# Token rows that move in 32-column groups: cluster similarities, softmax sums and gate logits of a routed-attention and expert kernel

## The chip, the cores and the metric

The kernel runs on one core of one Trainium2 chip. The metric is the device time of one launch in microseconds; lower is better. The core has TensorE (PE in the profile, with its weight loads as PEld), VectorE (DVE), ScalarE (ACT), GpSimd (POOL) and SyncE (SP, which issues most of the transfers). A program runs each engine's instructions in their written order. TensorE writes to PSUM, of which there are eight banks; the other engines copy from there.

## The reference

Two blocks follow each other. The first is attention with a mask from clustering: q, k and v have 4 batches, 8 heads, 768 tokens and 64 elements per head; each head has 16 centroids.

```
q_assign = argmax over c of  q_n . c_n      (k_assign likewise)
mask     = q_assign[:, None] == k_assign[None, :]
scores   = where(mask, q k^T / 8, -1e9);  attn = softmax(scores);  x = attn v
```

The second takes x as 3072 tokens of 512 elements and sends each to one of 8 experts:

```
logits = x @ w_gate                          (512 x 8)
e      = argmax(logits);  gate = softmax(logits)[e]
out    = gate * (relu(x @ w1[e]) @ w2[e])    (512 x 1024, 1024 x 512)
```

## The kernel before

All matrices are fp32. The attention stage works on 16 groups; a group is one batch and two heads, `a` = 0 and 1, which lie on partitions 0 to 63 and 64 to 127. A group has two halves of 384 queries, a half has six key blocks of 128, and a half with one key block is a unit: 12 units per group, 192 in all. `score(u)` computes the two heads' transposed scores of a unit (keys on partitions, 384 queries in the columns), adds the cluster mask by a bf16 product of one-hot tables, takes the exponential on ScalarE into `A`, and adds `A` into the sums tile `T` on VectorE. `attend(u)` multiplies `A` with v into the bank `O`, head `a` on partitions 64a to 64a+63.

The order is written out by hand. The loop steps two units at a time: two scores, two attends of two units earlier (LAG = 2), and then the jobs that a table `jobs` holds for the two units. A group's preparation begins 14 units ahead (LEAD): `turn` (three pieces of four transposes that bring q and k into `qk`, tokens in the columns), `similar` (the product with the normalized centroids, 12 matmuls, each with 128 tokens as the weights and 32 columns, so that tokens come out on partitions), `assign` and `assign2` (the first maximum as a one-hot row, on VectorE and GpSimd), `put` (six bf16 transposes for q and six for k, which bring the one-hot rows into `ohT`). `finish(g, half)` comes two units behind a half: it sums `T` over the keys with a matrix of ones, takes the reciprocal, multiplies `O` with it into `XT` (features on partitions, tokens in the columns), and adds up on GpSimd what a check of the range needs later. When the four groups of a batch are done, six `x_turn` jobs turn `XT` into token rows `X`, two `logits` jobs multiply `XT` with the gate matrix (12 matmuls each, 8 columns), `gate` computes the gate weight, and `keep_rows` writes the rows to DRAM from GpSimd's queue.

All jobs that need a PSUM bank for a short time take one of the two buffers called `mps` (pool `ps_m`); scores have four banks, `O` has two.

Behind the attention stage a chain of small VectorE operations and matmuls (from `sc`, L572, to `s_idx`, L676) sorts the tokens by expert. The expert stage gathers rows, turns them, and runs two layers per expert. The check of the range (L610 to L616) decides whether a general version of the whole kernel has to run behind this one; with the inputs here it does not.

Of the kernel before, what the change touches and what calls it, by code (L numbers as in the profile page):

```python
# [20 lines left out]
LAG = 2  # L21
# [161 lines left out]
def kernel(  # L183
# [11 lines left out]
    nc = tc.nc  # L195
    B, H, S, D = q.shape
    C = centroids.shape[1]
    P = 128
    NQ = S // P
# [10 lines left out]
    NT = N // P  # L210
    KA = D + C
    XW = Dm + 4
    assert D == 64 and H * C == P and NQ * P == S and DB * P == Dm and FB * P == F

    NJ = N // E // P
    CAP = NJ * P
# [30 lines left out]
    lmax = rte.tile([P, NT], F32)  # L247


    rsum = rte.tile([P, HS], F32)  # L250
    rlow = rte.tile([P, HS], F32)

    with ExitStack() as actx:
        ld = actx.enter_context(tc.tile_pool(name="ld", bufs=2))
# [7 lines left out]
        xtp = actx.enter_context(tc.tile_pool(name="xtp", bufs=5))  # L262
# [21 lines left out]
        wg = consts.tile([P, DB, E], F32)  # L284
        nc.scalar.dma_start(out=wg, in_=moe_w_gate.rearrange("(a p) e -> p a e", p=P))
# [6 lines left out]
        ones_h = consts.tile([P, D], F32)  # L292
        nc.gpsimd.memset(ones_h, 1.0)
        nc.gpsimd.memset(rsum, 0.0)
        nc.gpsimd.memset(rlow, 0.0)

        ohs = []
        for i in range(2):
# [52 lines left out]
                nc.scalar.copy(dst, src)  # L351

        def similar(g):
            ps = ps_m.tile([P, 512], F32, name="mps")
            for w in range(2):
                for j in range(NQ):
                    c0 = (w * NQ + j) * 2 * C
                    nc.tensor.matmul(  # L358
                        ps[:, c0 : c0 + 2 * C], lhsT=qk[g][:, w, j * P : (j + 1) * P],
                        rhs=cblk[:, g % HP].rearrange("p a c -> p (a c)"), start=True, stop=True,  # L360
                    )
            sims[g] = asg.tile([P, G, C], F32, name="sim")
            nc.scalar.copy(sims[g], ps[:, 0 : G * C].rearrange("p (t c) -> p t c", c=C))

        def assign(g):

            sim = sims.pop(g)
            mx = asg.tile([P, G], F32, name="mx")
            nc.vector.tensor_reduce(mx, sim, axis=AX, op=ALU.max)
            rank = asg.tile([P, G, C], F32, name="rank")  # L370
            nc.vector.tensor_tensor(rank, sim, mx.unsqueeze(2).to_broadcast([P, G, C]), op=ALU.is_ge)
            nc.gpsimd.tensor_tensor(rank, rank, first_c[:, None, :].to_broadcast([P, G, C]), op=ALU.mult)
            sims[g] = rank

        def assign2(g):
            rank = sims.pop(g)
# [7 lines left out]
        def put(g, w):  # L384
            if w == 0:
                ohT[g] = ohp.tile([P, 2, S], BF16, name="ohT")
            ps = ps_m.tile([P, 512], F32, name="mps").bitcast(BF16)
            for j in range(NQ):
                nc.tensor.transpose(
                    ps[:, j * P : (j + 1) * P], ohs[g % 2][:, w * NQ + j].rearrange("p a c -> p (a c)"), ident_b  # L390
                )
# [15 lines left out]
        def score(u):  # L407
            g, half, j = where(u)
            qs = slice(half * HS, (half + 1) * HS)
            ks = slice(j * P, (j + 1) * P)  # L410
            ps = ps_s.tile([P, 2, 512], F32, name="sps")
            for a in range(2):
                r = slice(a * D, (a + 1) * D)
                nc.tensor.matmul(ps[:, a, 0:HS], lhsT=qk[g][r, 1, ks], rhs=qk[g][r, 0, qs], start=True, stop=False)  # L414
            for a in range(2):
                r = slice(a * D, (a + 1) * D)
                nc.tensor.matmul(ps[:, a, 0:HS], lhsT=ohT[g][r, 1, ks], rhs=ohT[g][r, 0, qs], start=False, stop=True)  # L417
            A[u] = ap.tile([P, 2, HS], F32, name="A")
            nc.scalar.activation(A[u], ps[:, :, 0:HS], AF.Exp)  # L419
            if j == 1:  # L420
                T[g, half] = tp_.tile([P, 2, HS], F32, name="T")
                nc.vector.scalar_tensor_tensor(  # L422
                    T[g, half], in0=A[u - 1], scalar=1e-9 / P, in1=A[u], op0=ALU.add, op1=ALU.add
                )
            elif j > 1:
                nc.vector.tensor_tensor(T[g, half], T[g, half], A[u], op=ALU.add)  # L426
# [10 lines left out]
                )  # L437

        def finish(g, half):
            b, hp = divmod(g, HP)  # L440
            if half == 0:
                XT[b, hp] = xtp.tile([P, S], F32, name="xT")
            ps = ps_m.tile([P, 512], F32, name="mps")
            t = T.pop((g, half))
            for a in range(2):
                nc.tensor.matmul(  # L446
                    ps[a * D : (a + 1) * D, 0:HS], lhsT=ones_h, rhs=t[:, a, :], start=True, stop=True,
                )
# [10 lines left out]
        def x_turn(b, j):  # L459
            if j == 0:  # L460
# [3 lines left out]
            for c in range(DB):  # L464
                nc.tensor.transpose(ps[:, c * P : (c + 1) * P], XT[b, c][:, j * P : (j + 1) * P], ident)
            nc.scalar.copy(X[b][:, j, 0:Dm], ps)

        def logits(b, js):
            ps = ps_m.tile([P, 512], F32, name="mps")
            for i, j in enumerate(js):  # L470
                for c in range(DB):
                    nc.tensor.matmul(
                        ps[:, i * E : (i + 1) * E], lhsT=XT[b, c][:, j * P : (j + 1) * P], rhs=wg[:, c, :],
                        start=(c == 0), stop=(c == DB - 1),
                    )
            nc.vector.tensor_copy(
                lg[:, b * NQ + js[0] : b * NQ + js[-1] + 1, :],
                ps[:, 0 : len(js) * E].rearrange("p (j e) -> p j e", e=E),
            )

        def gate(b):
# [20 lines left out]
        def at(u, f, *a):  # L502
            jobs.setdefault(u, []).append((f, a))
# [3 lines left out]
        for g in range(NG):  # L507
            u0 = g * UG - LEAD
            for piece in range(3):
                at(u0 + piece, turn, g, piece)  # L510
            at(u0 + 4, similar, g)
            at(u0 + 5, assign, g)
            at(u0 + 7, assign2, g)
            at(u0 + 9, put, g, 0)
            at(u0 + 10, put, g, 1)
# [4 lines left out]
        for b in range(B):  # L520
            u0 = (b + 1) * HP * UG + LAG + 1
            for j in range(NQ):
                at(u0 + j, x_turn, b, j)
            at(u0 + 1, logits, b, (0, 1, 2))
            at(u0 + 3, logits, b, (3, 4, 5))
            at(u0 + 5, gate, b)
            at(u0 + 6, keep_rows, b)

        def early(e):
            weights[e] = fetch(e)  # L530
# [39 lines left out]
    with tc.tile_pool(name="sm", bufs=1) as sm, tc.tile_pool(name="rps", bufs=1, space=PSUM) as rps:  # L570
# [36 lines left out]
        )  # L607

        bad = sm.tile([P, 4], F32)
        nc.vector.tensor_reduce(bad[:, 0:1], rsum, axis=AX, op=ALU.max)  # L610
        nc.vector.tensor_reduce(bad[:, 1:2], rlow, axis=AX, op=ALU.max)
        nc.vector.tensor_scalar(bad[:, 0:1], bad[:, 0:1], scalar1=100.0, scalar2=None, op0=ALU.is_le)
        nc.vector.tensor_scalar(bad[:, 1:2], bad[:, 1:2], scalar1=0.5, scalar2=None, op0=ALU.is_le)
        nc.vector.tensor_tensor(bad[:, 2:3], bad[:, 0:1], bad[:, 1:2], op=ALU.mult)
# [187 lines left out]
```

## Time and profile before

| | us |
|---|---|
| median of three runs | 1006.79 |
| lowest and highest | 993.57, 1011.89 |
| the profiled execution, its own time | 1008.31 |
| its span in the trace | 1006.5 |
| attention stage, first score to last attend | 20.28 to 498.90 |
| last attend to the first routing operation (`sc`) | 498.90 to 515.64 |
| first weight load of the expert layers | 547.64 |

All times in the trace count from the start of the span. A fp32 matmul appears as two records of MATMUL, a fp32 transpose as one. Records of matmuls overlap, so the cost of a piece of PE work is best read from its start to the start of the next work of another kind. The granted clock is given as a share of TensorE's full speed (1.0 is 2.4 GHz, 0.5 is 1.2 GHz). A number in square brackets behind an instruction is the idle time of its engine ahead of it, and what ended that.

### The profile page before, as it was taken

The numbers are of one execution on the slowest core, as the hardware profiler recorded it, in microseconds if no ns is written. First come the engines' busy times: TensorE is split into PE (matmuls) and PEld (weight loads), VectorE is DVE, ScalarE is ACT, GpSimd is POOL, SyncE is SP. The second block draws the span as 40 slices with busy tenths as digits, with TensorE's granted clock in tenths as the row PEclk, the third lists the DMA queues.
The fourth block names the chain that finished last, engine by engine and source line by source line (L and its number), as shares of the span: only waits on it lengthen the run. The fifth ranks groups of instructions, "written<-read, shape, count | busy, mean of one in ns | idle before, by whom it ended". The sixth has DMA issues, their size and how long they took to land. (4 is left out here: it accounts for less than half of the span.)

```text
span 1006.5 us, 11290 instructions
## 1 busy us (share of the span) xinstructions
PE 941.5 (94%) x4655; PEld 525.4 (52%) x4655; DVE 386.2 (38%) x493; ACT 257.1 (26%) x392; POOL 210.8 (21%) x218
## 2 busy tenths in 40 slices
PE   5999999999999999999967999999999999988896
PEld 4555555454555555555365555545455454555664
DVE  2677745677447775477752101011010100000110
ACT  4444434444334443344410010101100010010100
POOL 3133321333113332132323020101201011010100
PEclk8999989999789998899955999999999999998998
DMA  7016223161221612100012242324334233446610
GB/s 166 16 41 214 49 48 109 32 199 35 48 80 32 215 48 48 73 7 1 1 63 64 83 145 97 133 105 160 141 128 146 100 131 125 159 165 223 236 62 9
DMA packets 82587, 99.02 MB, mean 98 GB/s; under 512 B 52959, under 2 KB 57055, under 8 KB 82016
## 3 DMA queue, kind: packets, MB, share of 16 engines
q1 hardware_dynamic: 76480, 77.60, 24.9%
q0 software_dynamic: 5376, 20.56, 5.2%
q8 instruction: 39, 0.64, 0.3%
q14 instruction: 20, 0.16, 0.1%
q10 hardware_dynamic: 672, 0.05, 0.0%
HBM read 85.57 MB, written 14.20 MB: 99 GB/s over the span
## 5 line engine op out<-in xcount | busy, mean ns | idle before, releaser
L706 PE MATMUL hp<-xgT,w 128*128 128x384 f32 (+1 forms) x896 | 212.9, 399 | 0.8 <-DVE xgT L698 0.8
L719 PE MATMUL zp<-w,h_sb 128*128 128x512 f32 x480 | 211.2, 599 | 0.0
L419 ACT ACTIVATE A<-sps 128x768 f32<-128x768 f32 x192 | 155.2, 811 | 110.9 <-PE sps L417 106.7
L414 PE MATMUL sps<-qk 64*128 64x384 f32 x768 | 183.1, 557 | 0.4 <-ACT A L419 0.4
L706 PEld LDWEIGHTS hp<-xgT,w 128*128 128x128 f32 x896 | 142.4, 193 | 74.2 <-issue 8.6
L426 DVE TENSOR_TENSOR T<-T,A 128x768 f32<-128x768 f32 x128 | 133.9, 1046 | 88.8 <-ACT A L419 82.7
L711 DVE TENSOR_SCALAR h_sb<-hp 128x384 f32<-128x384 f32 (+1 forms) x56 | 24.8, 444 | 359.2 <-PE hp L706 359.2
L434 PE MATMUL O<-A,v_in 128*64 128x384 f32 x768 | 149.7, 512 | 0.0
L719 PEld LDWEIGHTS zp<-w,h_sb 128*128 128x128 f32 x480 | 91.4, 193 | 109.8 <-issue 109.8
L725 POOL DMA_INDIRECT out_dram<-zo,s_idx x30 | 30.1, 1002 | 391.5 <-ACT zo L724 378.5
L454 POOL TENSOR_TENSOR rsum<-rsum,rd 128x384 f32<-128x384 f32 x32 | 32.0, 1000 | 333.0 <-DVE rd L450 333.0
L434 PEld LDWEIGHTS O<-A,v_in 128*64 128x64 f32 x768 | 48.4, 141 | 89.0 <-issue 88.9
L414 PEld LDWEIGHTS sps<-qk 64*128 64x128 f32 x768 | 69.6, 203 | 46.9 <-issue 25.6
L450 DVE RECIPROCAL rd<-mps 128x384 f32<-128x384 f32 x32 | 81.8, 2557 | 3.2 <-PE mps L446 2.1
L724 ACT ACTIVATE zo<-zp,xg 128x512 f32<-128x512 f32 x30 | 20.6, 687 | 222.1 <-PE zp L719 222.1
L713 ACT ACTIVATE h_sb<-hp 128x384 f32<-128x384 f32 (+1 forms) x56 | 22.3, 399 | 214.8 <-PE hp L706 214.8
L417 PE MATMUL sps<-ohT 64*128 64x384 bf16 x384 | 69.0, 352 | 0.0
L358 PEld LDWEIGHTS mps<-cblk,qk 128*128 128x128 f32 x384 | 44.3, 193 | 9.2 <-issue 9.2
L455 POOL TENSOR_SCALAR rd<-rd 128x384 f32<-128x384 f32 x32 | 45.9, 1433 | 2.8
L422 DVE SCALAR_TENSOR_TENSOR T<-A 128x768 f32<-128x768 f32 x32 | 31.2, 976 | 39.6 <-ACT A L419 39.6
L358 PE MATMUL mps<-cblk,qk 128*128 128x32 f32 x384 | 46.0, 278 | 0.0
L697 PE MATMUL tp<-ident,xg 128*128 128x128 f32 x120 | 19.3, 298 | 21.2 <-DMA xg<-x_rows,g_idx 18.8
(140 smaller groups left out, 556.0 us busy)
## 6 DMA issues: line engine op xcount, KB each, us to landing
w<-in_moe_w_dram SPq DMA_DIRECT2D x28, 2048.0 KB, 9.4
x_rows<-x POOLq DMA_DIRECT2D x4, 1548.0 KB, 5.5
q_in<-in_q_dram SPq DMA_DIRECT2D x32, 192.0 KB, 4.4
k_in<-in_k_dram SPq DMA_DIRECT2D x32, 192.0 KB, 4.7
v_in<-in_v_dram SPq DMA_DIRECT2D x16, 384.0 KB, 3.3
xg<-x_rows,g_idx POOLq DMA_INDIRECT x30, 6.9
out_dram<-zo,s_idx POOLq DMA_INDIRECT x30, 2.7
csb<-in_centroids_dram ACTq DMA_DIRECT2D x1, 32.0 KB, 1.9
```

The lines of the kernel that those rows point to most:

```text
L358: nc.tensor.matmul(ps[:, c0 : c0 + 2 * C], lhsT=qk[g][:, w, j * P : (j + 1) * P], rhs=cblk[:, g % HP].rearrange("p a c -> p (a c)"), start ...
L414: nc.tensor.matmul(ps[:, a, 0:HS], lhsT=qk[g][r, 1, ks], rhs=qk[g][r, 0, qs], start=True, stop=False)
L417: nc.tensor.matmul(ps[:, a, 0:HS], lhsT=ohT[g][r, 1, ks], rhs=ohT[g][r, 0, qs], start=False, stop=True)
L419: nc.scalar.activation(A[u], ps[:, :, 0:HS], AF.Exp)
L422: nc.vector.scalar_tensor_tensor(T[g, half], in0=A[u - 1], scalar=1e-9 / P, in1=A[u], op0=ALU.add, op1=ALU.add)
L426: nc.vector.tensor_tensor(T[g, half], T[g, half], A[u], op=ALU.add)
L434: nc.tensor.matmul(O[g, half][a * D : (a + 1) * D, 0:HS], lhsT=rows[g, "v"][:, a, j, :], rhs=a_[:, a, :], start=(j == 0), stop=(j == NQ - 1),)
L450: nc.vector.reciprocal(rd, ps[:, 0:HS])
L454: nc.gpsimd.tensor_tensor(rsum, rsum, rd, op=ALU.add)
L455: nc.gpsimd.tensor_scalar(rd, rd, scalar1=1e-30, scalar2=None, op0=ALU.is_lt)
L706: nc.tensor.matmul(hp[:, :cols], lhsT=g["w"][0][:, c, fb * P : (fb + 1) * P], rhs=g["xT"][:, c, :cols], start=(c == 0), stop=(c == DB - 1),)
L719: nc.tensor.matmul(zp, lhsT=g["h"][:, fb, j * P : (j + 1) * P], rhs=g["w"][1][:, fb, :], start=(fb == 0), stop=(fb == FB - 1),)
```

## The change

The tokens become the moving operand in `similar` and in the logits. `similar` now uses the centroids (32 columns) as weights and 384 tokens as the moving columns, four matmuls whose outputs go to partitions 0, 32, 64 and 96; the result is copied to `simT`, and a new job `similar2` turns it back with three transposes. `finish` only copies `O` to `XT`. A new job `weigh` computes, with weights of 32 columns, the two heads' sums (rows 16 and 17) and the logits per head before division (rows 0 to 15) in one bank, a half on partitions 0 to 31 and the other on 32 to 63. `weigh2` turns that to token rows, takes the reciprocal there, and adds the divided logits up over groups. `x_turn` now runs per group and half with three transposes and divides on VectorE as it copies out of PSUM. The check of the range reads the collected sums `dens`.

```diff
-            ps = ps_m.tile([P, 512], F32, name="mps")
-            for w in range(2):
-                for j in range(NQ):
-                    c0 = (w * NQ + j) * 2 * C
-                    nc.tensor.matmul(
-                        ps[:, c0 : c0 + 2 * C], lhsT=qk[g][:, w, j * P : (j + 1) * P],
-                        rhs=cblk[:, g % HP].rearrange("p a c -> p (a c)"), start=True, stop=True,
-                    )
+            ps = ps_m.tile([P, 512], F32, name="mps")
+            for t in range(4):
+                w, half = divmod(t, 2)
+                nc.tensor.matmul(
+                    ps[t * 2 * C : (t + 1) * 2 * C, 0:HS], lhsT=cblk[:, g % HP].rearrange("p a c -> p (a c)"),
+                    rhs=qk[g][:, w, half * HS : (half + 1) * HS], start=True, stop=True,
+                )
+            sims[g] = asg.tile([P, HS], F32, name="simT", bufs=1)
+            nc.scalar.copy(sims[g], ps[:, 0:HS])
+
+        def similar2(g):
+            simT = sims.pop(g)
+            ps = ps_m.tile([P, 512], F32, name="mps")
+            for i in range(NQ // 2):
+                nc.tensor.transpose(ps[:, i * P : (i + 1) * P], simT[:, i * P : (i + 1) * P], ident)
             sims[g] = asg.tile([P, G, C], F32, name="sim")
...
         def finish(g, half):
+            if half == 0:
+                XT[g] = xtp.tile([P, S], F32, name="xT")
+            nc.scalar.copy(XT[g][:, half * HS : (half + 1) * HS], O.pop((g, half))[:, 0:HS])
...
+        def weigh(g):
+            ps = ps_m.tile([P, 512], F32, name="mps")
+            t = [T.pop((g, half)) for half in range(2)]
+            for i in range(3):
+                for half in range(2):
+                    nc.tensor.matmul(
+                        ps[half * 32 : (half + 1) * 32, 0:HS],
+                        lhsT=one_row[:, i, :] if i < 2 else wg[:, g % HP, :],
+                        rhs=t[half][:, i, :] if i < 2 else XT[g][:, half * HS : (half + 1) * HS],
+                        start=(i == 0), stop=(i == 2),
+                    )
+            lsT[g] = stat.tile([64, HS], F32, name="lsT", bufs=1)
+            nc.scalar.copy(lsT[g], ps[0:64, 0:HS])
+
+        def weigh2(g):
...
+            for i in range(NQ // 2):
+                nc.tensor.transpose(ps[:, i * 64 : (i + 1) * 64], lt[:, i * P : (i + 1) * P], ident[0:64, 0:64])
+            ls = stat.tile([P, NQ, 32], F32, name="ls")
+            nc.vector.tensor_copy(ls, ps[:, 0 : NQ * 32].rearrange("p (t r) -> p t r", r=32))
+            den = ls[:, :, 2 * E : 2 * E + 2]
+            rds[g] = stat.tile([P, NQ, 2], F32, name="rd")
+            nc.vector.reciprocal(rds[g], den)
...
-            rd = stat.tile([P, HS], F32, name="rd")
-            nc.vector.reciprocal(rd, ps[:, 0:HS])
             nc.vector.tensor_tensor(
-                XT[b, hp][:, half * HS : (half + 1) * HS], O.pop((g, half))[:, 0:HS], rd, op=ALU.mult
-            )
-            nc.gpsimd.tensor_tensor(rsum, rsum, rd, op=ALU.add)
-            nc.gpsimd.tensor_scalar(rd, rd, scalar1=1e-30, scalar2=None, op0=ALU.is_lt)
-            nc.gpsimd.tensor_tensor(rlow, rlow, rd, op=ALU.add)
...
+            at(u0 + 6, similar2, g)
+            at(u0 + 7, assign, g)
+            at(u0 + 8, assign2, g)
+            at(u0 + 10, put, g, 0)
+            at(u0 + 11, put, g, 1)
...
+        for g in range(NG):
+            u1 = (g + 1) * UG + LAG
+            at(u1 + 2, weigh, g)
+            at(u1 + 4, weigh2, g)
+            at(u1 + 5, x_turn, g, 0)
+            at(u1 + 8, x_turn, g, 1)
+            if g % HP == HP - 1:
+                at(u1 + 6, gate, g // HP)
+                at(u1 + 9, keep_rows, g // HP)
```

`wg` becomes a padded table of 32 columns that GpSimd fills from the loaded gate matrix at the start, behind the load and ahead of the memsets of the one-hot tables.

## Rows read from the trace of the kernel before

**Rows 1.** The page, section 1: busy time, share of the span, instructions of each engine.
```profile
PE 941.5 (94%) x4655; PEld 525.4 (52%) x4655; DVE 386.2 (38%) x493; ACT 257.1 (26%) x392; POOL 210.8 (21%) x218
```
**Rows 2.** Windows: from:to, length, busy us per engine, then granted clock, DMA.
```profile
20.28:498.90 478.62, 467.77 (x2973) 244.27 (x2972) 314.26 (x331) 204.84 (x289) 132.29 (x113) 0.93 0.24 69
29.26:55.38 26.12, 26.12 (x177) 13.34 (x177) 19.30 (x20) 12.23 (x17) 4.83 (x5) 1.00 0.20 46
498.90:515.64 16.74, 13.94 (x74) 12.62 (x73) 6.31 (x13) 2.34 (x4) 5.43 (x6) 0.68 0.00 0
```
**Rows 3.** Timeline of TensorE, full clock: start, length, line, operation.
```profile
32.52 0.92 PE L414 MATMUL sps<-qk 64*128 64x384 f32 x4
...
34.34 1.51 PE L434 MATMUL O<-A,v_in 128*64 128x384 f32 x8
35.78 0.51 PE L389 MATMUL mps<-ident_b,oh 128*128 128x128 bf16 x6
36.22 0.92 PE L414 MATMUL sps<-qk 64*128 64x384 f32 x4
...
43.82 0.87 PE L338 MATMUL mps<-ident,q_in 128*128 128x128 f32 x6
...
44.84 0.92 PE L414 MATMUL sps<-qk 64*128 64x384 f32 x4
...
48.10 0.66 PE L338 MATMUL mps<-ident,k_in 128*128 128x128 f32 x4
48.68 0.92 PE L414 MATMUL sps<-qk 64*128 64x384 f32 x4
...
51.84 0.82 PE L446 MATMUL mps<-T,ones_h 128*64 128x384 f32 x4
52.59 2.87 PE L358 MATMUL mps<-cblk,qk 128*128 128x32 f32 x24
55.38 0.92 PE L414 MATMUL sps<-qk 64*128 64x384 f32 x4
...
448.95 0.88 PE L338 MATMUL mps<-ident,q_in 128*128 128x128 f32 x6
```
**Rows 4.** Timeline of TensorE: `similar` and what follows, twice.
```profile
78.87 2.87 PE L358 MATMUL mps<-cblk,qk 128*128 128x32 f32 x24
81.66 1.64 PE L414 MATMUL sps<-qk 64*128 64x384 f32 x4
...
85.16 1.51 PE L434 MATMUL O<-A,v_in 128*64 128x384 f32 x8
...
457.72 2.87 PE L358 MATMUL mps<-cblk,qk 128*128 128x32 f32 x24
460.52 1.62 PE L414 MATMUL sps<-qk 64*128 64x384 f32 x4
```
**Rows 5.** Groups by line and shape: count, busy us, mean ns, idle before.
```profile
L706 PE MATMUL hp<-xgT,w 128*128 128x384 f32 x512 | 169.1, 492 | 0.8 <-DVE xgT L698 0.8
L434 PE MATMUL O<-A,v_in 128*64 128x384 f32 x768 | 149.7, 512 | 0.0
L450 DVE RECIPROCAL rd<-mps 128x384 f32<-128x384 f32 x32 | 81.8, 2557 | 3.2 <-PE mps L446 2.1
L472 PE MATMUL mps<-wg,xT 128*128 128x8 f32 x192 | 27.0, 280 | 0.7 <-ACT x L466 0.7
L451 DVE TENSOR_TENSOR xT<-O,rd 128x384 f32<-128x384 f32 x32 | 17.8, 557 | 1.1
L363 ACT COPY sim<-mps 128x384 f32<-128x384 f32 x16 | 7.6, 478 | 62.6 <-PE mps L358 62.6
```
**Rows 6.** Timeline around the end of the attention stage, TensorE and VectorE.
```profile
503.83 4.28 PE L472 MATMUL mps<-wg,xT 128*128 128x8 f32 x24 [0.68 <-ACT x L466]
509.73 5.29 PE L472 MATMUL mps<-wg,xT 128*128 128x8 f32 x24
515.64 0.35 DVE L572 TENSOR_TENSOR sc<-lg,lmax 128x192 f32<-128x192 f32 x1
```
**Rows 7.** Timeline of TensorE in a batch end, a transpose that waited.
```profile
161.82 0.66 PE L465 MATMUL mps<-ident,xT 128*128 128x128 f32 x4 [2.22 <-DVE rd L450]
```

More of the change, by code (lines that the diff above doesn't have):

```diff
@@ L212 @@
     XW = Dm + 4
-    assert D == 64 and H * C == P and NQ * P == S and DB * P == Dm and FB * P == F
+    assert D == 64 and C == 16 and H * C == P and NQ % 2 == 0 and NQ * P == S and DB * P == Dm and FB * P == F
     NJ = N // E // P
@@ L247 @@
     lmax = rte.tile([P, NT], F32)
-    rsum = rte.tile([P, HS], F32)
-    rlow = rte.tile([P, HS], F32)
+    dens = rte.tile([P, NG, 2 * NQ], F32)
     with ExitStack() as actx:
@@ L261 @@
         xp = actx.enter_context(tc.tile_pool(name="xp", bufs=1))
-        xtp = actx.enter_context(tc.tile_pool(name="xtp", bufs=5))
+        xtp = actx.enter_context(tc.tile_pool(name="xtp", bufs=2))
         ps_s = actx.enter_context(tc.tile_pool(name="ps_s", bufs=2, space=PSUM))
@@ L283 @@
         nc.scalar.dma_start(out=csb, in_=centroids.rearrange("h c d -> (h c) d"))
-        wg = consts.tile([P, DB, E], F32)
-        nc.scalar.dma_start(out=wg, in_=moe_w_gate.rearrange("(a p) e -> p a e", p=P))
+        wg_in = consts.tile([P, DB, E], F32)
+        nc.scalar.dma_start(out=wg_in, in_=moe_w_gate.rearrange("(a p) e -> p a e", p=P))
         load(0)
@@ L291 @@
         first_e = iota("first_e", [P, E], [[-1, E]], E, 0)
[L292 to L295, printed above, removed]
+        wg = consts.tile([P, DB, 32], F32)
+        nc.gpsimd.memset(wg, 0.0)
+        one_row = consts.tile([P, 2, 32], F32)
+        nc.gpsimd.memset(one_row, 0.0)
+        for a in range(2):
+            r = slice(a * D, (a + 1) * D)
+            nc.gpsimd.tensor_copy(wg[r, :, a * E : (a + 1) * E], wg_in[r])
+            nc.gpsimd.memset(one_row[:, a, 2 * E + a : 2 * E + a + 1], 1.0)
         ohs = []
@@ L354, in similar @@
             ps = ps_m.tile([P, 512], F32, name="mps")
-            for w in range(2):
-                for j in range(NQ):
-                    c0 = (w * NQ + j) * 2 * C
-                    nc.tensor.matmul(
-                        ps[:, c0 : c0 + 2 * C], lhsT=qk[g][:, w, j * P : (j + 1) * P],
-                        rhs=cblk[:, g % HP].rearrange("p a c -> p (a c)"), start=True, stop=True,
-                    )
+            for t in range(4):
[11 more added lines that the diff above has]
+                nc.tensor.transpose(ps[:, i * P : (i + 1) * P], simT[:, i * P : (i + 1) * P], ident)
             sims[g] = asg.tile([P, G, C], F32, name="sim")
-            nc.scalar.copy(sims[g], ps[:, 0 : G * C].rearrange("p (t c) -> p t c", c=C))
+            nc.scalar.copy(sims[g], ps[:, 0:HS].rearrange("p (t c) -> p t c", c=C))
         def assign(g):
@@ L369, in assign @@
             nc.vector.tensor_reduce(mx, sim, axis=AX, op=ALU.max)
[L370 to L373, printed above, removed]
+            nc.vector.tensor_tensor(sim, sim, mx.unsqueeze(2).to_broadcast([P, G, C]), op=ALU.is_ge)
+            nc.gpsimd.tensor_tensor(sim, sim, first_c[:, None, :].to_broadcast([P, G, C]), op=ALU.mult)
+            sims[g] = sim
         def assign2(g):
@@ L389, in put @@
                 nc.tensor.transpose(
[L390 removed]
+                    ps[:, j * P : (j + 1) * P], ohs[g % 2][:, (j % (NQ // 2)) * 4 + w * 2 + j // (NQ // 2)].rearrange("p a c -> p (a c)"), ident_b
                 )
@@ L420, in score @@
             if j == 1:
-                T[g, half] = tp_.tile([P, 2, HS], F32, name="T")
+                T[g, half] = tp_.tile([P, 2, HS], F32, name="T", bufs=3)
                 nc.vector.scalar_tensor_tensor(
@@ L439, in finish @@
         def finish(g, half):
+            if half == 0:
+                XT[g] = xtp.tile([P, S], F32, name="xT")
+            nc.scalar.copy(XT[g][:, half * HS : (half + 1) * HS], O.pop((g, half))[:, 0:HS])
+        lsT, rds = {}, {}
+        def weigh(g):
[11 more added lines that the diff above has]
+            nc.scalar.copy(lsT[g], ps[0:64, 0:HS])
@@ L440, in finish @@
+        def weigh2(g):
             b, hp = divmod(g, HP)
-            if half == 0:
-                XT[b, hp] = xtp.tile([P, S], F32, name="xT")
+            lt = lsT.pop(g)
             ps = ps_m.tile([P, 512], F32, name="mps")
[L444 to L447, printed above, removed]
-                )
-            rd = stat.tile([P, HS], F32, name="rd")
@@ L451, in finish @@
+            nc.gpsimd.tensor_copy(dens[:, g, :].rearrange("p (t a) -> p t a", a=2), den)
+            lgh = stat.tile([P, NQ, 2, E], F32, name="lgh")
             nc.vector.tensor_tensor(
-                XT[b, hp][:, half * HS : (half + 1) * HS], O.pop((g, half))[:, 0:HS], rd, op=ALU.mult
-            )
-            nc.gpsimd.tensor_tensor(rsum, rsum, rd, op=ALU.add)
-            nc.gpsimd.tensor_scalar(rd, rd, scalar1=1e-30, scalar2=None, op0=ALU.is_lt)
-            nc.gpsimd.tensor_tensor(rlow, rlow, rd, op=ALU.add)
@@ L459, in x_turn @@
-        def x_turn(b, j):
-            if j == 0:
+                lgh, ls[:, :, 0 : 2 * E].rearrange("p t (a e) -> p t a e", a=2),
+                rds[g].unsqueeze(3).to_broadcast([P, NQ, 2, E]), op=ALU.mult,
+            )
+            lgb = lg.rearrange("p (b h i) e -> p b i h e", b=B, h=2)[:, b]
+            lgv = lgh.rearrange("p (i h) a e -> p i h a e", h=2)
+            if hp == 0:
+                nc.vector.tensor_tensor(lgb, lgv[:, :, :, 0, :], lgv[:, :, :, 1, :], op=ALU.add)
+            else:
+                for a in range(2):
+                    nc.vector.tensor_tensor(lgb, lgb, lgv[:, :, :, a, :], op=ALU.add)
@@ L461, in x_turn @@
+        def x_turn(g, half):
+            b, hp = divmod(g, HP)
+            if hp == 0 and half == 0:
                 X[b] = xp.tile([P, NQ, XW], F32, name="x")
@@ L463, in x_turn @@
             ps = ps_m.tile([P, 512], F32, name="mps")
[L464 to L468, printed above, removed]
-            ps = ps_m.tile([P, 512], F32, name="mps")
[L470 to L478, printed above, removed]
+            n = NQ // 2
+            for i in range(n):
+                nc.tensor.transpose(
+                    ps[:, i * P : (i + 1) * P], XT[g][:, (half * n + i) * P : (half * n + i + 1) * P], ident
+                )
+            nc.vector.tensor_tensor(
+                X[b][:, half * n : (half + 1) * n, hp * P : (hp + 1) * P].rearrange("p i (a d) -> p i a d", a=2),
+                ps[:, 0 : n * P].rearrange("p (i a d) -> p i a d", i=n, a=2),
+                rds[g].rearrange("p (i h) a -> p i h a", h=2)[:, :, half, :].unsqueeze(3).to_broadcast([P, n, 2, D]),
+                op=ALU.mult,
             )
@@ L511 @@
             at(u0 + 4, similar, g)
[L512 to L515, printed above, removed]
+            at(u0 + 6, similar2, g)
[3 more added lines that the diff above has]
+            at(u0 + 11, put, g, 1)
             for half in range(2):
@@ L519 @@
             at((g - 2) * UG + LAG + 2, load, g)
[L520 to L527, printed above, removed]
+        for g in range(NG):
[7 more added lines that the diff above has]
+                at(u1 + 9, keep_rows, g // HP)
         def early(e):
@@ L609 @@
         bad = sm.tile([P, 4], F32)
[L610 to L614, printed above, removed]
+        fit = sm.tile([P, NG * 2 * NQ], F32)
+        den = dens.rearrange("p g t -> p (g t)")
+        nc.vector.tensor_scalar(fit, den, scalar1=0.01, scalar2=None, op0=ALU.is_ge)
+        nc.vector.scalar_tensor_tensor(fit, in0=den, scalar=1e30, in1=fit, op0=ALU.is_le, op1=ALU.mult)
+        nc.vector.tensor_reduce(bad[:, 2:3], fit, axis=AX, op=ALU.min)
         bps = rps.tile([P, 1], F32, name="bps")
```

## The prediction

> **What bounds the kernel now.** I read the page's first section, then the windows of the stages, then the timeline of TensorE alone. The page shows TensorE (PE) at 94% of the span and no other engine above 52% [rows 1]. The windows say where a saving counts: from the first score to the last attend (20.28 to 498.90) PE is busy 467.77 of 478.62 us, and in a stretch of full clock 26.12 of 26.12, while VectorE has 19.30 and ScalarE 12.23 of those 26.12 [rows 2]. So in this stage each us of PE work is a us of time, idle PE is 10.85 us in all, and the granted clock, 0.93 in the mean, is the third thing paid for. The expert stage behind it is not touched. The gap from the last attend to the first routing step, 16.74 us, is a latency chain.
>
> The timeline gives PE's prices at full clock, each from one start to the next, so that what a change of work costs is in it [rows 3]. A pair of units (two scores, two attends) is 35.78 - 32.52 = 3.26 us, of which the scores take 34.34 - 32.52 = 1.82. Six bf16 transposes of `put` take 0.44. Four fp32 transposes take 48.68 - 48.10 = 0.58 and eight 44.84 - 43.82 = 1.02, so one is 0.11 and going there and back 0.14. The two sum matmuls of `finish` take 0.75, `similar` 55.38 - 52.59 = 2.79.
>
> The stage built of these: 96 pairs 313, turns 23, `similar` 15 x 2.79 = 41.9, `put` 15 x 0.88 = 13.2, sums 31 x 0.75 = 23.3, 18 `x_turn` pieces 10.4, the logits of three batches 17.4 (below): 442. With 10.9 idle it is 453; the 25.5 left to 478.6 are what half clock took. (The clock row alone would say 0.07 x 478.6 = 33.5; some of that fell on small matmuls.) In a fall the granted clock is 0.5, 1.2 of 2.4 GHz. After `similar` the next score pair takes 85.16 - 81.66 = 3.50 and not 1.82: 1.68 lost. This follows 10 of the 15 `similar` from 26.47 on, the first and last of the ten in [rows 4]; the other falls sit in the batch ends, among `x_turn` and `logits`.
>
> **The change, part by part.** Its own time is 1008.31 us, 1.5 above the median 1006.79.
>
> *Similarities.* Twelve matmuls with 128x128 weights and 32 columns go; four with 32-column weights and 384 columns come, on four column groups, then three transposes a pair later. No row has 32-column groups. The nearest is `attend`: a full 128x128 matmul of 384 columns costs 169.1/256 = 0.66 us, but two in two 64-column groups together also cost 0.75 at most (`sums`), and 384 of them 149.7, 0.39 each [rows 5, 3]. Two groups run at once, and 0.75 - 0.11 = 0.64 is what such a set of 384 columns costs beside the going there and back. If four do, the four matmuls cost 0.75; if two at a time 1.39; one at a time 4 x 0.64 + 0.11 = 2.67. I take 0.75, since both halves of the array were seen to run apart. Transposes 3 x 0.11 + 0.14 = 0.47. Per group -2.79 + 1.22 = -1.57, 15 groups: **-23.6**. The first group's `similar` lies ahead of the stage; its gain there goes into the new copy and transposes: 0. POOL's queue there gains two copies of `wg` that wait for its load, with the `oh` and `cblk` memsets behind them, in place of three memsets; first needed by `similar`, behind three turns: 0.
>
> *Sums and logits.* Per group two sum steps of 0.75 go. Six matmuls come in three pairs: 3 x 0.64 + 0.11 = 2.03 (one at a time 3.95), and three transposes, at most 0.47 (64 rows, bounded by the full ones). +1.00 x 15: **+15.0**. The old logits: 192 records, 27.0 us, less the two pieces at the end of 4.28 and 5.29 [rows 5, 6]: **-17.4**. `x_turn` keeps 96 transposes, in pieces of three beside other pieces: 15 x 6 x 0.11 = 9.9 for 10.4, 0. `keep_rows` issues one transfer per batch as before, some units later on POOL's queue; the next thing behind it there that uses its tile is the memset of the next batch, eight units on: 0. SP's queue keeps its order.
>
> *Vector, scalar, POOL.* Reciprocal (2.56) and product (0.56 [rows 5]) twice per group become small operations on 128x192 and less, and two products of 0.56 out of PSUM; VectorE falls from 19.3 towards 16 per group. ScalarE gains two copies of 0.48 [rows 5] per group for `finish`, two for `simT` and `lsT`, and loses `x` copies; some 14 of the new group's 27 us. POOL loses three operations per half. Behind `weigh2` VectorE holds seven operations ahead of the next additions, and ScalarE's exponentials need a free `A` of four; the additions come back in line within a pair. All of it lies beside PE; without that cover the new hand-offs (0.48 four times, some 2 us of VectorE after `weigh2`, 1 us for buffers) would show as 5.2 us a group, a rival below.
>
> *Waits.* The batch ends hold PE for `lg` and `rd`, one for 2.22 us [rows 7]; these 10.9 us go. A new one: at units 10 and 11 of a group `turn`, `x_turn` and `turn` want three of two PSUM buffers, and the third waits for VectorE's copy of the first, queued behind two T additions: PE gets there after 3.26 and seven transposes with their going back, some 3.9 to 4.2 us into the pair. VectorE's second addition ends at about 3.65 (two scores 1.8, an exponential 0.8, an addition 1.0), its copy 0.7 later, at 4.35. I take 0.4 (ends 0 and the 2.22 of that row), 15 times. **-10.9 + 6.0 = -4.9**. Behind the waiting transposes stand the next scores; ScalarE waits for them.
>
> *Clock.* Stretches without long matmuls shrink. The 1.02 us of turns was never followed by a fall (14 stretches, the first at 43.82 and the last at 448.95 [rows 3]), the 2.79 of `similar` in 10 of 15. The longest new one, turns with `x_turn` and the wait, is 11 x 0.11 + 0.14 + 0.4 = 1.75, between them, nearer the turns: I take 3 falls in 15 (ends 0 and 15). **-25.5 + 3 x 1.68 = -20.5**.
>
> The Trainium skill (TensorE: Matmul & The Clock Gate, Part 4: PE-mode transpose) says that transposes don't count as a busy PE for the clock, which speaks against spreading more of them. By it every turn stretch of the new kernel would lose the clock, and the sum would be 966 instead of 946; the rows of the turns don't bear it out at 1.02 us, and none shows 1.75.
>
> *End.* Now 16.74 from the last attend to `sc` at 515.64 [rows 2, 6]. Then: `weigh` 2.0, copy 0.5, transposes 0.5, some seven small VectorE operations and one of 0.56, 3.0 together: 6.0 (ends 5 and 9). **-10.7**.
>
> Sum: -23.6 + 15.0 - 17.4 - 4.9 - 20.5 - 10.7 = -62.1; 1008.3 - 62.1 = 946 on the profiled execution, 945 against the median.
>
> **Rivals.**
> *Two column groups at a time.* `similar` costs 1.39: +0.64 x 15 = 9.6, 956. For it: the rows show two, never four. 0.12.
> *The clock falls at each turn stretch*: 12 more falls x 1.68 = 20, 966. For it: 1.75 is nearer to the falling stretches than any turn was. Against: 0 of 14. 0.13. (The rule above, of the Trainium skill's page on the clock gate, would make this the forecast.)
> *The 32-column groups don't run at once*: 1.92 for `similar` and 1.92 for `weigh`, 15 times, and at the end: +59.5, 1006, no change. The change then doesn't do what it says. Against: the 64-column rows. 0.06.
> *Hand-offs uncovered*: ScalarE and VectorE fall behind and PE waits 5.2 instead of 0.4 per group: +72, 1018, still within 2%. Against: 16 and 14 of 27 us of work. 0.05.
> *Slower*: PE leaves its long matmuls five times per group (`similar`; `similar2` and `weigh`; `weigh2` and `x_turn`; `put`; turns), and each costs half clock in the next pair. At four falls a group it is (60 - 3) x 1.68 = +96, 1042; it decides from 3.4 falls a group, (1027 - 946 + 5)/1.68/15. For it: falls do follow stretches of transposes in the batch ends. Against: `put` and turn stretches today, and long matmuls in two of the five. 0.04.
>
> **How the numbers follow.** The forecast, 0.60, is the likeliest: 945. What a measurement can tell from no change here is 2%, 20 us (the three runs span 993.57 to 1011.89). Faster holds the forecast and the first two rivals: 0.85; same the next two: 0.11; slower 0.04. The low end has no falls, no new wait and the 33.5 of the clock row in place of 25.5: 945 - 5 - 6 - 8 = 926, taken as 928 since not all meet; the high end has the turn falls together with pairs only: 945 + 20 + 10 = 975, 976. A wait at its upper end (+27) lies inside. These hold 0.85, of which I count 0.8 in.
>
> **What would show it.** `similar` near 0.75 from its start to the next PE work, and 15 of them with no half-speed scores behind; `weigh` near 2.0; no `logits` line; PE's stage from first score to last attend near 427 us with clock above 0.97; `turn` idle before its third piece near 0.4; the first routing step 6 us after the last attend. Matmul records of the four groups that start one after another, or a stage mean of the clock still at 0.93, would make it wrong.

## The result, and the profile after

The changed kernel takes 941.83 us (median of four runs, 938.9 to 943.67) where the kernel before took 1005.37 in the same comparison: a ratio of 0.940, 95% interval 0.931 to 0.949. The forecast was 945. The profiled execution takes 942.97 us, its span is 941.1; against the 1008.31 and 1006.5 of before that is 65.3 us less, where the sum of the prediction had 62.1.

The page's first section answers to [rows 1]. PE's share is what it was, 94%: it is still the bound, with 61 us less to do. VectorE lost 84 us and GpSimd 118.

```profile
PE 880.3 (94%) x4367; PEld 454.3 (48%) x4367; DVE 302.1 (32%) x527; ACT 270.8 (29%) x432; POOL 93.2 (10%) x141
```

The windows answer to [rows 2] (from:to, length, busy us by engine, granted clock, DMA): the stage from first score to last attend, one group in it, and the stretch up to just behind the start of the first routing operation.

```profile
21.65:445.87 424.22, 417.96 (x2754) 187.13 (x2753) 233.43 (x365) 220.56 (x332) 19.98 (x37) 1.00 0.27 78
28.71:55.15 26.44, 26.44 (x179) 11.83 (x175) 14.13 (x18) 15.54 (x23) 1.00 (x1) 1.00 0.21 45
445.87:451.90 6.03, 3.93 (x25) 1.78 (x23) 2.60 (x14) 0.95 (x2) 0.19 (x1) 1.00 0.00 0
```

The stage fell from 478.62 to 424.22 us, and its granted clock rose from 0.93 to 1.00. PE's idle time in it is 6.26 us and was 10.85. VectorE's work per group fell to 14 us, ScalarE's rose to 16; neither is near the length of a group.

The timeline of TensorE through one group answers to [rows 3] (start, length, line, operation; a piece's price is the distance to the next start shown).

```profile
51.11 0.85 PE L362 MATMUL mps<-qk,cblk 128*32 128x384 f32 x8
51.90 0.92 PE L425 MATMUL sps<-qk 64*128 64x384 f32 x4
...
55.15 0.55 PE L373 MATMUL mps<-ident,simT 128*128 128x128 f32 x3
55.63 1.48 PE L463 MATMUL mps<-T,one_row 128*32 128x384 f32 x8
...
57.69 0.92 PE L425 MATMUL sps<-qk 64*128 64x384 f32 x4
...
60.95 0.40 PE L477 MATMUL mps<-ident,lsT 64*128 64x64 f32 x3
61.27 0.55 PE L506 MATMUL mps<-ident,xT 128*128 128x128 f32 x3
61.75 0.92 PE L425 MATMUL sps<-qk 64*128 64x384 f32 x4
...
69.04 0.65 PE L342 MATMUL mps<-ident,q_in 128*128 128x128 f32 x4
69.53 0.49 PE L506 MATMUL mps<-ident,xT 128*128 128x128 f32 x3
70.48 0.44 PE L342 MATMUL mps<-ident,q_in 128*128 128x128 f32 x2 [0.46 <-DVE qk L350]
...
71.07 0.92 PE L425 MATMUL sps<-qk 64*128 64x384 f32 x4
```

`similar` takes 0.78 us where it took 2.79, its transposes 0.48, `weigh` 2.06, `weigh2` 0.33. Eight records of four matmuls in 0.78 us are four column groups at once: one such matmul over the whole array costs 0.66 [rows 5]. The same timeline from 51.10 to 51.14 has the first records of all four in flight, so they do not go one after another, which the prediction had named as a sign of being wrong.

```profile
51.11 0.53 PE L362 MATMUL mps<-qk,cblk 128*32 128x384 f32 x4
```

The turns with `x_turn` take 2.03, of which 0.46 are the wait for a buffer that VectorE still reads.

At the end the last attend is done at 445.87 and `sc` starts at 451.83: 5.96 us, and it was 16.74 [rows 2, 6]. This is the line of VectorE's timeline:

```profile
451.83 0.35 DVE L609 TENSOR_TENSOR sc<-lg,lmax 128x192 f32<-128x192 f32 x1
```

One part got longer. The first score starts at 21.65 and not at 20.28. The timeline of the start shows the chain: GpSimd waits for the load of `wg_in`, then clears the one-hot tables and only then `cblk`; VectorE's copy into `cblk` waits for that, and the second turn piece waits for the PSUM buffer from which that copy reads.

```profile
4.71 0.20 POOL L298 COPY wg<-wg_in 64x32 f32<-64x32 f32 x1 [1.85 <-DMA wg_in<-in_moe_w_gate_dram]
...
8.03 0.20 POOL L328 MEMSET cblk<- 128x128 f32 x1
...
8.26 0.46 DVE L331 COPY cblk<-mps 64x64 f32<-64x64 f32 x2 [1.49 <-POOL cblk L328]
...
8.87 0.66 PE L342 MATMUL mps<-ident,q_in 128*128 128x128 f32 x2 [0.65 <-DVE cblk L331]
```

### The profile page after: what moved, and what is told of

Read it like the earlier page. It is cut to its first block, busy times and chain, and to the rows that moved or that the text cites. A ratio compares the mean times of both kernels' runs of the same rounds, so it can differ in the third digit from the quotient of the medians.

```text
span 941.1 us, 10715 instructions
## 1 busy us (share of the span) xinstructions
PE 880.3 (94%) x4367; PEld 454.3 (48%) x4367; DVE 302.1 (32%) x527; ACT 270.8 (29%) x432; POOL 93.2 (10%) x141
## 4 chain that ended last, share of the span: by engine, by line
issue 44%; PE 40%; DVE 7%; POOL 6%; ACT 1%; DMA 0%; POOLq 0%; DVEq 0%; ACTq 0%
PE sps L425 14%; PE O L445 12%; PE mps L463 4%; DVE T L437 3%; PE sps L428 3%; POOL out_dram L762 3%; POOL xg L724 3%; PE mps L342 2%; PE mps L362 1%; ACT A L430 1%; PE tok_ps L703 1%; PE mps L400 1%; DVE qk L350 1%; PE mps L373 1%; PE mps L506 1%
## 5 line engine op out<-in xcount | busy, mean ns | idle before, releaser
L425 PE MATMUL sps<-qk 64*128 64x384 f32 x768 | 166.1, 510 | 0.0
L437 DVE TENSOR_TENSOR T<-T,A 128x768 f32<-128x768 f32 x128 | 122.5, 957 | 85.6 <-ACT A L430 78.6
L445 PE MATMUL O<-A,v_in 128*64 128x384 f32 x768 | 145.1, 499 | 0.0
L748 DVE TENSOR_SCALAR h_sb<-hp 128x384 f32<-128x384 f32 (+1 forms) x56 | 24.9, 444 | 358.9 <-PE hp L743 358.9
L425 PEld LDWEIGHTS sps<-qk 64*128 64x128 f32 x768 | 63.4, 187 | 52.2 <-issue 31.5
L750 ACT ACTIVATE h_sb<-hp 128x384 f32<-128x384 f32 (+1 forms) x56 | 22.3, 399 | 215.3 <-PE hp L743 215.3
L428 PE MATMUL sps<-ohT 64*128 64x384 bf16 x384 | 63.2, 323 | 0.0
L383 POOL TENSOR_TENSOR sim<-sim,first_c 128x384 f32<-128x384 f32 x16 | 15.9, 994 | 300.6 <-DVE sim L382 300.6
L735 DVE COPY xgT<-tp 128x512 f32<-128x512 f32 x30 | 20.1, 689 | 45.5 <-PE tp L734 45.5
L428 PEld LDWEIGHTS <-ohT 64*128 64x128 bf16 x384 | 19.4, 94 | 24.9 <-issue 0.3
L724 POOL DMA_INDIRECT xg<-x_rows,g_idx x30 | 29.1, 971 | 16.3 <-issue 8.8
L734 PEld LDWEIGHTS tp<-ident,xg 128*128 128x128 f32 x120 | 14.9, 153 | 25.2 <-issue 19.3
```

Source lines behind the costliest of these rows:

```text
L445: nc.tensor.matmul(O[g, half][a * D : (a + 1) * D, 0:HS], lhsT=rows[g, "v"][:, a, j, :], rhs=a_[:, a, :], start=(j == 0), stop=(j == NQ - 1),)
L724: nc.gpsimd.indirect_dma_start(out=g["xg"][:, j, :], out_offset=None, in_=x_d[:, :], in_offset=bass.IndirectOffsetOnAxis(ap=g["gi"](j), ax ...
L734: nc.tensor.transpose(tp[:, c, :], g["xg"][:, j, c * P : (c + 1) * P], ident)
```

## The experiments

Three questions were open: how much of the gain belongs to the similarities and to the clock, what made the clock fall in the kernel before, and whether VectorE's lost work matters. All runs were timed in three rounds beside the kernel before; the medians are given, and the stage is the window from first score to last attend of the profiled execution. A fall of the clock is a stretch at a granted clock of 0.5 that begins in the stage. By this count the kernel before has 15: ten behind `similar`, and five in or behind five of the six rows of `logits` in its stage, 12 matmuls of 8 columns each.

| run | median us | ratio to before, 95% interval | stage us | falls of the clock in it |
|---|---|---|---|---|
| the change | 941.83 | 0.931 to 0.949 | 424.22 | 0 |
| similar alone | 964.76 | 0.958 to 0.976 | 434.74 | 1 |
| similar undone | 976.76 | 0.968 to 0.986 | 457.30 | 6 |
| 20 transposes more | 975.14 | 0.967 to 0.984 | 456.37 | 0 |
| 32 transposes more | 994.34 | 0.979 to 0.990 | 476.70 | 0 |
| 10 narrow matmuls more | 976.00 | 0.969 to 0.986 | 457.87 | 0 |
| 12 narrow matmuls more | 995.55 | 0.981 to 0.993 | 472.71 | 5 |
| x_turn apart | 934.33 | 0.922 to 0.938 | 414.75 | 0 |
| reciprocal back | 966.71 | 0.952 to 0.970 | 446.54 | 2 |
| reciprocal back, x_turn apart | 936.35 | 0.924 to 0.940 | 417.59 | 0 |
| four more in one column group | 987.41 | 0.974 to 0.992 | 462.55 | 0 |
| weigh in four groups | 933.43 | 0.918 to 0.928 | 415.46 | 0 |
| all three | 923.28 | 0.909 to 0.920 | 405.08 | 0 |

### Similar alone

The new `similar`, `similar2`, their order and the in-place `assign` in the kernel before.

```diff
 kernel before
...
-                        ps[:, c0 : c0 + 2 * C], lhsT=qk[g][:, w, j * P : (j + 1) * P],
+                    ps[t * 2 * C : (t + 1) * 2 * C, 0:HS], lhsT=cblk[:, g % HP].rearrange("p a c -> p (a c)"),
...
+            at(u0 + 6, similar2, g)
...
```

> The kernel before with the new similar, similar2 and their times in the order alone; sums, logits and x_turn as before. My theory: 15 times 2.79 becomes 0.78 + 0.48, -23.0, and the ten falls of the clock after similar go with it, 10 x 1.68 = -16.8: about 40 us below the kernel before, some 965; the half-speed stretches at the batch ends stay. Rival 1, the falls belong to the rhythm of the stage and only move elsewhere: -23, some 982. Rival 2, without the new sums the new copies on ScalarE and the busy VectorE (reciprocals still there) make PE wait: 985 or more.

The time came out, 964.76, but one part of the expectation did not. The window of the stage:

```profile
20.68:455.42 434.74, 417.05 (x2778) 198.78 (x2777) 320.86 (x331) 212.40 (x304) 128.72 (x113) 0.99 0.26 76
```

The clock is 0.99, and one fall is left in the whole stage, at 138.03 in a row of `logits`, which TensorE's timeline shows:

```profile
135.52 3.04 PE L479 MATMUL mps<-wg,xT 128*128 128x8 f32 x24 [0.19 <-ACT sim L371]
```

The half-speed stretches of the other batch ends went too, although their `x_turn` and `logits` jobs are those of before; why is not shown. PE's idle time grew from 10.85 to 17.69 us, since both `put` jobs and, at the batch ends, `x_turn` now meet in one pair and wait for ScalarE's copies. PE's busy time fell by 50.7 us: 23.0 of matmul work, and about 28 that half clock had cost. So the similarities alone bring 43.9 of the stage's 54.4 us.

### Similar undone

The old `similar` in the changed kernel.

```diff
 changed kernel
...
-                    ps[t * 2 * C : (t + 1) * 2 * C, 0:HS], lhsT=cblk[:, g % HP].rearrange("p a c -> p (a c)"),
+                        ps[:, c0 : c0 + 2 * C], lhsT=qk[g][:, w, j * P : (j + 1) * P],
...
-            at(u0 + 6, similar2, g)
...
```

> The changed kernel with the old similar put back (twelve matmuls of 32 columns, one copy, the old tile order), all else changed. My theory: +23.0 for the matmuls and +17 for some ten falls of the clock behind them: about 982, with half-clock stretches of one score pair after about 10 of 15 similar and nowhere else in the stage. Rival, the falls of the kernel before came from its batch ends and general waiting: +23, 965, clock 1.0.

It took 976.76, 34.9 above the changed kernel. That is 23.0 of work, six falls of 1.68, 10.1, and a first score at 24.04 instead of 21.65, 2.4 (the first `similar`, ahead of the stage, ran at half clock and took 5.30): together 35.5. The falls stand behind `similar` and nowhere else in the stage, six and not ten; here is one in TensorE's timeline.

```profile
199.79 2.87 PE L362 MATMUL mps<-cblk,qk 128*128 128x32 f32 x24
202.58 1.15 PE L417 MATMUL sps<-qk 64*128 64x384 f32 x4
...
203.84 1.50 PE L417 MATMUL sps<-qk 64*128 64x384 f32 x4
```

### Transposes or narrow matmuls

Two kernels of equal length: 20 more transposes, or 10 more matmuls of the old form, ahead of the third turn piece; then the same with 32 and 12. All of it is overwritten.

```diff
 changed kernel, in turn
+            if piece == 2 and g > 0:
+                for i in range(20):
+                    nc.tensor.transpose(ps[:, 0:P], rows[g, "q"][:, i % NQ].rearrange("p a d -> p (a d)"), ident)
```

```diff
 changed kernel, in turn
+            if piece == 2 and g > 0:
+                for i in range(10):
+                    nc.tensor.matmul(
+                        ps[:, 0 : 2 * C], lhsT=qk[g][:, 0, 0:P],
+                        rhs=cblk[:, g % HP].rearrange("p a c -> p (a c)"), start=True, stop=True,
+                    )
```

> The changed kernel with 20 more fp32 transposes (results overwritten) ahead of the four of the third turn piece, 15 groups: a stretch of 0.59 + 20 x 0.11 = 2.8 us without long matmuls, as long as the old similar. My theory (transposes keep the clock, the small matmuls of the old similar lost it): +33 for the work, no falls, 975. Rival, the rule that transposes don't count as a busy PE: about ten falls more, +17, 992.

> The changed kernel with 10 matmuls in the form of the old similar (128x128 weights, 32 columns, results overwritten) ahead of the four transposes of the third turn piece, 15 groups: 0.59 + 10 x 0.224 = 2.8 us, the same length as in the run with transposes. My theory: +34 for the work and about ten falls of 1.68, 992. Rival, any stretch of this length does the same: this run and the one with transposes have the same clock.

The transposes did what I expected: 975.14, no fall. The narrow matmuls did not: 976.00 and no fall either, so my theory in that form was wrong, and so far the rival held, since both runs had the same clock. TensorE's timeline and the window of the stage, with ten:

```profile
78.97 2.42 PE L342 MATMUL mps<-cblk,qk 128*128 128x32 f32 x20
81.22 0.64 PE L348 MATMUL mps<-ident,k_in 128*128 128x128 f32 x4
81.78 0.92 PE L431 MATMUL sps<-qk 64*128 64x384 f32 x4
```

```profile
21.67:479.54 457.87, 451.59 (x3055) 220.53 (x3056) 233.43 (x365) 220.82 (x332) 20.03 (x37) 1.00 0.25 72
```

But this rival could not explain the run with `similar` undone, where twelve such matmuls lost the clock six times. One difference was the length of the narrow part, 2.25 us against 2.79. So the next two runs made both longer.

> As the run with 10 narrow matmuls (2.25 us of them, no fall of the clock), with 12, as many as the old similar, in the same place: 2.7 us of them, then the four transposes. My theory now: small matmuls lose the clock, but only where enough of them stand in a row, and transposes don't: 12 x 0.224 x 15 = +40 for the work and falls behind 6 to 10 of 15, +10 to 17: 992 to 999. Rival, what loses the clock is what stands around the old similar (sums or scores), not these matmuls: 982, no falls.

> As the run with 20 transposes (no fall), with 32: 4.1 us in a row without a long matmul, more than any stretch of the old similar. My theory: transposes keep the clock, +32 x 0.11 x 15 = 53, 995, no falls in the stage. Rival, transposes count less and 20 were too few: a fall behind nearly each, +25, 1020.

With twelve narrow matmuls the falls are back, behind 5 of 15 of these stretches, 995.55 us, and the mean granted clock of whole executions agrees: 0.973 in all four with ten, 0.956 to 0.964 in the four with twelve. The timeline shows one fall:

```profile
139.99 2.87 PE L342 MATMUL mps<-cblk,qk 128*128 128x32 f32 x24
142.69 0.64 PE L348 MATMUL mps<-ident,k_in 128*128 128x128 f32 x4
143.25 1.60 PE L431 MATMUL sps<-qk 64*128 64x384 f32 x4
```

With 32 transposes, 4.1 us together with the four that follow, there is none: 994.34 us, and the clock of the stage is 1.00. Its timeline and its window:

```profile
81.35 3.71 PE L342 MATMUL mps<-ident,q_in 128*128 128x128 f32 x32
84.90 0.60 PE L345 MATMUL mps<-ident,k_in 128*128 128x128 f32 x4
85.43 0.92 PE L428 MATMUL sps<-qk 64*128 64x384 f32 x4
```

```profile
21.62:498.32 476.70, 470.45 (x3235) 239.39 (x3236) 233.34 (x365) 220.71 (x332) 19.98 (x37) 1.00 0.24 70
```

So rows of small matmuls lose the clock, twelve of them in some places and ten in none, and transposes do not, up to 36 in a row. They are not the only cause: two falls of the next section stand at waits of TensorE. The rule that was weighed in the prediction (the Trainium skill, TensorE: Matmul & The Clock Gate, Part 4: PE-mode transpose), that transposes don't count as a busy PE in the way of other work, does not hold here: 36 fp32 transposes in a row kept 2.4 GHz in each of 15 groups. Why the clock fell behind some rows of twelve and not behind others was not tried further.

### The third buffer, and VectorE's work

Two units later for the second `x_turn`; and, in both orders, VectorE's reciprocal put back with an unused result.

```diff
 changed kernel
-            at(u1 + 8, x_turn, g, 1)
+            at(u1 + 10, x_turn, g, 1)
...
-                at(u1 + 9, keep_rows, g // HP)
+                at(u1 + 11, keep_rows, g // HP)
...
```

```diff
 changed kernel, in finish
+            junk = stat.tile([P, HS], F32, name="junk")
+            nc.vector.reciprocal(junk, T[g, half][:, 0, :])
```

> The changed kernel with the second x_turn of a group two units later (unit 0 of the next group, beside the third turn piece, keep_rows moved along), so that no pair wants three of the two PSUM buffers. My theory: the 0.65 us that turn, x_turn and turn take above their transposes goes, 14 times: -9, 933. Rival, the wait moves to another buffer use: 942.

> The changed kernel with a VectorE reciprocal of 128x384 put back into each finish (of one half of T, result unused): VectorE's load of the kernel before without its place in the chain. My theory: VectorE goes from 14 to 19 of 27 us, and where it runs late, in the pair before the turns, the third buffer comes some 1.3 us later, 14 times: +18, 960. Rival 1, hidden: 942. Rival 2, T and A come late everywhere: 980.

> The same reciprocal with the second x_turn two units later. My theory: without the pair that wants three buffers VectorE's load is hidden, 933 as without it. Rival, T or A come late: 950.

With `x_turn` apart the time is 934.33, and PE has no idle time left in the stage:

```profile
21.67:436.42 414.75, 414.75 (x2751) 187.13 (x2750) 234.27 (x364) 220.72 (x332) 20.03 (x37) 1.00 0.27 80
```

The stage fell by 9.5 us, 14 times 0.68: the wait of 0.46 and 0.22 more of PE's busy time (414.75 where it was 417.96). The reciprocal, which puts back 74 us of VectorE's work, cost 24.9 us in the order of the change, 966.71, where I had expected 960. The waits of PE name the place (who waits, for whom: us in total, times, longest): the third buffer, 21.0 us in this kernel and 6.3 in the changed one.

```profile
PE mps L342 <- DVE qk L350: 21.0, 13, 2.0
```

```profile
PE mps L342 <- DVE qk L350: 6.3, 13, 0.7
```

That is 14.7; the rest of the stage's 22.3 are two falls of the clock and shorter waits. The falls, at 214.80 and 272.83, stand at this third buffer, with no row of small matmuls ahead: TensorE waits 1.61 us at the one, 0.68 and 1.98 at the other. The timeline at the first, and its window:

```profile
213.98 0.44 PE L342 MATMUL mps<-ident,q_in 128*128 128x128 f32 x2 [1.61 <-DVE qk L350]
```

```profile
214.80:218.22 3.42, 3.42 (x14) 1.35 (x14) 0.00 (x0) 1.57 (x4) 0.00 (x0) 0.50 0.00 0
```

With `x_turn` apart the same reciprocal cost 2.0 us, 936.35, and neither fall is there. So the 82 us of VectorE's reciprocals were not on the path by their sum; they would have been by one pair of units, in which VectorE's lateness holds a buffer that PE needs.

### One column group, and four in weigh

```diff
 changed kernel, in similar
+            for t in range(4):
+                w, half = divmod(t, 2)
+                nc.tensor.matmul(
+                    ps[0 : 2 * C, 0:HS], lhsT=cblk[:, g % HP].rearrange("p a c -> p (a c)"),
+                    rhs=qk[g][:, w, half * HS : (half + 1) * HS], start=True, stop=True,
+                )
```

> The changed kernel with four more matmuls in similar, all into the same 32-column group (partitions 0 to 31), overwritten by the four that count. My theory: the four run at once because each has a column group of its own; in one group they go one after another, 4 x 0.64 = 2.6 us, 16 times: +41, 983. Rival, the narrow weights alone let matmuls overlap: +0.64 x 16, 952.

The time is 987.41. In TensorE's timeline `similar` now takes 59.49 - 56.15 = 3.34, 2.56 more, which is four times 0.64:

```profile
56.15 2.44 PE L362 MATMUL mps<-qk,cblk 128*32 128x384 f32 x7
58.12 0.52 PE L368 MATMUL mps<-qk,cblk 128*32 128x384 f32 x3
...
58.46 1.10 PE L368 MATMUL mps<-qk,cblk 128*32 128x384 f32 x5
59.49 0.92 PE L431 MATMUL sps<-qk 64*128 64x384 f32 x4
```

In one group the narrow matmuls go one behind the other, at the price of a full one; so narrow weights alone don't let four run at once, separate column groups do. (A column group and its output rows in PSUM go together here, and the four added ones overwrite the same rows: no run tells the two apart.) `weigh` uses two of four. The last two runs use all: sums in two groups, logits in the other two.

```diff
 changed kernel, in weigh
-            for i in range(3):
+            for i in (0, 2, 1):
                 for half in range(2):
+                    blk = (i // 2) * 2 + half
                     nc.tensor.matmul(
-                        ps[half * 32 : (half + 1) * 32, 0:HS],
+                        ps[blk * 32 : (blk + 1) * 32, 0:HS],
...
-                        start=(i == 0), stop=(i == 2),
+                        start=(i != 1), stop=(i > 0),
...
```

> The changed kernel with weigh on four column groups: the sums of the two halves in groups 0 and 1, the logits of the two halves in groups 2 and 3, so two steps of 384 columns and not three; lsT has 128 rows and ls is a copy of 384 columns. My theory: weigh 2.06 becomes 1.42, weigh2 at most 0.15 more: 15 x 0.5 to 0.64 and once at the end, -8 to -10, 933. Rival, VectorE's and ScalarE's larger copies or a wait for XT take it back: 942.

> Four column groups in weigh, the second x_turn two units later, and GpSimd's memsets of cblk and the one-hot tables ahead of its copies of wg. My theory: the parts add up: 942 - 9 (four groups) - 7.5 (x_turn, as measured) - 1 (start): 924. Rival, four groups only shift a wait: 934.

Four groups alone give 933.43, and all three edits (four groups, `x_turn` apart, and the memsets of the start moved ahead) 923.28: a ratio of 0.915 to the kernel before (0.909 to 0.920), and 0.980 of the change's median. In the run with all three the timeline shows `weigh` at 56.43 - 55.02 = 1.41 and the sums and logits in flight together; the window shows PE busy in all of the stage.

```profile
55.02 0.52 PE L463 MATMUL mps<-T,one_row 128*32 128x384 f32 x2
55.03 0.52 PE L463 MATMUL mps<-xT,wg 128*32 128x384 f32 x2
...
55.69 0.81 PE L463 MATMUL mps<-T,one_row 128*32 128x384 f32 x4
56.43 0.92 PE L424 MATMUL sps<-qk 64*128 64x384 f32 x4
```

```profile
20.79:425.87 405.08, 405.08 (x2751) 184.88 (x2750) 237.03 (x364) 220.58 (x332) 19.97 (x37) 1.00 0.28 82
```

Its first score starts at 20.79: the memsets ahead of the copies of `wg` gave 0.86 of the 1.37 back. The nine profiles with the start and the `similar` of the change lie between 21.62 and 22.42.

## Why the prediction was right

| step | forecast | measured | from |
|---|---|---|---|
| similar | -23.6 | -23.0 | 15 x (0.78 + 0.48 - 2.79) |
| sums | +15.0 | +13.4 | 15 x (2.06 + 0.33 - 1.50) |
| logits | -17.4 | -17.4 | no such line is left |
| waits of PE | -4.9 | -4.6 | 6.26 and 10.85 idle |
| clock | -20.5 | -25.5 | clock 1.00: all of the forecast's 25.5 |
| start | 0 | +1.4 | 21.65 and 20.28 |
| end | -10.7 | -10.8 | 5.96 and 16.74 |
| behind `sc` | 0 | -1.6 | 489.27 and 490.86 us to the end of the span |

The measured column gives -68.1 and the spans differ by 65.4. The stage alone fell by 54.4 where these rows of it give 57.1, a difference of 2.7 us. The 3.2 us of busy time that went with the third buffer's wait in the run with `x_turn` apart (417.96 to 414.75) would cover it; the joins of pieces were not counted one by one. The stretch behind `sc` lasts from 486.8 to 494.8 us in the profiles of this document, so its -1.6 says nothing.

That the sum came within 3.3 us of the span's fall owes something to luck: the clock gave 5.0 us more than forecast, the sums cost 1.6 less and the stretch behind `sc` was 1.6 shorter, while the start, `similar`, the waits and these 2.7 us took 5.0 back.

*Work.* The prices from start to start held within 0.03 us for `similar`, its transposes and `weigh`; `weigh2`, put at 0.47 at most, took 0.33. For the 32-column groups, which no row showed, 0.75 was taken from two groups and 0.78 was measured; the run with one group shows that the groups are the reason. The first and the third rival, two at a time and none at a time, are out.

*Clock.* This is the step that was sized wrong, on the good side. Three falls were counted and none came. The second rival, a fall behind each turn stretch, is out: these stretches last 2.03 us, longer than the 1.75 that I had put down, and none of the 14 lost the clock. The reading behind it, that the length of a stretch without long matmuls decides, was wrong: the runs with 20 and 32 transposes have longer ones and no fall, and twelve narrow matmuls are enough. The prediction gave the batch ends' falls a place and no cause: they sit in or behind rows of `logits`, again twelve small matmuls, which the change takes away. Replacing `similar` alone left one of those five falls; why the other four went with it is open. The last rival, half clock after each change of work, is out as well.

*Waits.* The 0.4 us for the third buffer were 0.46, at the place named. The price of that pair was larger, 0.68, as the run with `x_turn` apart shows.

*Cover.* The hand-offs cost nothing beyond that wait, as forecast. That VectorE's relief is worth nothing was said too plainly: with nearly its old load the change would have been 24.9 us slower in this order of jobs.

*Start.* Costed at nothing, and 1.4 us. Some 1.1 of it is the wait: `similar` starts at 10.74 and not at 9.64, because the copies of `wg` waited 1.85 us for their load, and `cblk` behind them was late for VectorE's copy, which holds a PSUM buffer. The rest goes with the new copy and transposes of the first group, which were put at 0: with `similar` alone changed, the first score starts at 20.68, 0.4 late. I had asked when `similar` needs `cblk` and not who else holds what until `cblk` is there.

## What to carry to other kernels

Where TensorE is the bound, price each piece from its start to the start of the next kind of work and count pieces; here that gave the stage to 3 us in 424. A matmul that has few useful output rows should be given narrow weights and a column group of its own, so that its neighbours run beside it: four in 0.78 us against twelve in 2.79. And look for pairs of jobs that want more buffers than there are: that is where work of an engine off the path comes back on it.

## What was not expected of the hardware

- Rows of small matmuls lower the granted clock and transposes don't: 12 fp32 matmuls of 32 columns were followed by half clock in 10, 6 and 5 of 15 places (three kernels), 10 of them in none, 36 transposes in none. Waits of TensorE did it too: of the 13 at the third buffer with the reciprocal put back, two, of 1.61 and 1.98 us, stand at a fall; without these waits, and with the same reciprocal, there is none.
- The kernel before is as uneven as its clock. Of the runs beside these experiments its shortest, 991.47 us, had a mean granted clock of 0.956, and its longest, 1014.55, had 0.934; the changed kernel's four lie between 938.9 at 0.973 and 943.67 at 0.969.
- Four fp32 matmuls of 384 columns with 32-column weights take 0.78 us from start to start in four column groups and 2.56 more when four others share one group.
